# Two half-wide d_ff tiles in one PSUM bank, and three small moves of work between engines

## The chip, the cores and the metric

The kernel runs on one core of one Trainium2 chip. The metric is the device time of one execution in microseconds (us). The core has five engines with instruction streams of their own: TensorE (PE, with its weight loads shown as PEld), VectorE (DVE), ScalarE (ACT), GpSimd (POOL) and SyncE (SP), which here only issues transfers. Each works through its own stream in order and waits for the others through semaphores. TensorE writes its results to PSUM, from where ScalarE or VectorE must fetch them.

## The reference

Attention within chunks of 64 tokens, then a feed-forward layer with a squared relu (8 batches, 8 heads, 576 tokens a batch, head size 64; 4608 tokens, d_model 512, d_ff 2048):

```python
# q, k, v: [8, 8, 576, 64], cut into chunks of 64 tokens
scores = scale * q_c @ k_c.T          # within a chunk, scale = 1/8
attn = softmax(scores)
x = (attn @ v_c)                      # laid out as [4608 tokens, 512]
h = np.maximum(x @ w_in, 0.0)         # [4608, 2048]
out = (h * h) @ w_out                 # [4608, 512], float32
```

## The kernel before

Tokens are taken in 18 groups of 256 (`GT`), two groups to a block, so nine blocks of 512 tokens. For each block the kernel runs a feed-forward expansion (`ffn_in`) and a contraction (`ffn_out`, or `ffn_out_by_ft` in block 0). All products are in bf16.

**Expansion.** `ffn_in` goes over tiles of 128 columns of d_ff. A tile takes a bank of PSUM (`ps_ffn`, four buffers), four matmuls over d_model, a relu on ScalarE into the buffer `rl` (three buffers), and a square into `gT`. The square runs on VectorE, for a few named tiles on ScalarE (`SQUARES_ON_ACT`, `SQUARES_ON_ACT_EARLY`), so as to share the load. In blocks 2 to 8 a tile is 512 tokens wide and the tiles follow the order `FT_EARLY`: 8, 0, 9, 1, 10 to 15, 2 to 7, so tile 7 is the last. In block 1 the second group of tokens isn't ready when the block starts, so the tiles are 256 tokens wide: 16 tiles for the first group, 16 for the second, in the order 8 to 15, 0 to 7 (`FT_ORDER`).

**Contraction.** `ffn_out` multiplies with a scheme of seven products over quarters of `gT` and `w_out` (Strassen's, in Winograd's manner of sharing). It needs the differences d5, d2, d1, d6 and d7 of quarters of `gT`, which VectorE computes into `w_st` (the line of `difference`), and sums of quarters of `w_out`, made once (`sum_quarters`). The products use the order a22, a11, d5, d2, d1, d6, d7; d5 needs all of tiles 0 to 15 for the first group of tokens, tile 7 with them.

**Attention between the matmuls.** The attention of later groups is put into the blocks by a plan written by hand. Each `yield` of the expansion and the contraction ends a slot, and after slot s the plan emits the pieces listed for it. The pieces of a group are: C, which casts q and k to bf16 (`cast_qk`, on GpSimd for groups below 8, on ScalarE after); TD, which transposes them with a DMA on SP's queue; TA, TQ and TK, which transpose them on TensorE for the early groups; SC, scores and exp (`scores`); AV, the product with v and the division by the sum (`values`), whose reciprocal and multiplication are on VectorE and make `x`; XT, the transpose of x into `xT`, from which `ffn_in` reads (on TensorE for groups 2 to 5, by DMA later). Loads of q, k and v are issued on SP at the slots named in `go_slots`. As SP is in order, a load that is emitted behind a TD starts only after it, and TD waits for the casts of C.

In block 0's plan, TA, SC, AV and XT of group 2 stand at slots 24, 27, 29 and 31; slots 16 to 27 are `ffn_out_by_ft`'s tiles 0 to 11, slots 28 to 31 its last four token tiles. In block 1's plan, TK, SC, AV and XT of group 3 stand at slots 1, 4, 7 and 12, C of groups 4 and 5 at slots 16 and 20, TD at 21 and 27, their SC at 36 and 37 and AV at 38 and 40. From block 2 on, the two AV of the next block's groups stand near slots 11 and 15, which is the last slot of the expansion.

Of the kernel before, what the change touches and what calls it, by code (L numbers as in the profile page):

```python
# [10 lines left out]
FP32 = mybir.dt.float32  # L11
BF16 = mybir.dt.bfloat16
AF = mybir.ActivationFunctionType
ALU = mybir.AluOpType
# [3 lines left out]
def kernel(  # L18
# [9 lines left out]
    nc = tc.nc  # L28
# [24 lines left out]
    FIRST_DMA_T = 4  # L53
    FIRST_DMA_X = 6
    SQUARES_ON_ACT = (10, 14, 3)
    SQUARES_ON_ACT_EARLY = (9, 10, 12)
    BT = GT * max(len(b) for b in blocks)

    const_pool = ctx.enter_context(tc.tile_pool(name="const", bufs=1))
# [5 lines left out]
    ps_ffn = ctx.enter_context(tc.tile_pool(name="ps_ffn", bufs=4, space=bass.MemoryType.PSUM))  # L65
# [90 lines left out]
    def go(pieces):  # L156
        for f in pieces:
            f()
# [94 lines left out]
    def cast_qk(g):  # L253
        qkb = att_pool.tile([128, 2, 2 * H * D], BF16, name="qkb", bufs=2)
        state["qkb", g] = qkb

        copy = nc.gpsimd.tensor_copy if g < 8 else nc.scalar.copy
        q_sb, k_sb = (x.rearrange("p t h d -> p (t h d)") for x in qk[g])
        copy(  # L259
            out=qkb[:, 0].rearrange("p (i h d) -> p i h d", i=2, h=H),  # L260
            in_=q_sb.rearrange("p (h i d) -> p i h d", h=H, i=2))
        copy(out=qkb[:, 1], in_=k_sb)  # L262
# [90 lines left out]
    SC, AV, XT = scores, values, transpose_x  # L353
# [25 lines left out]
    def difference(j, name, part):  # L379
        if (name, j) not in state:  # L380
            state[name, j] = wst_pool.tile([128, 1024], FP32, name="w_st").bitcast(BF16).rearrange(
                "p (a f) -> p a f", a=HF)
        x, y = (quarters(j)[i][:, part] for i in DIFFERENCES[name])
        nc.vector.tensor_tensor(out=state[name, j][:, part], in0=x, in1=y, op=ALU.subtract)  # L384
# [4 lines left out]
    FT_EARLY = [ft + h for ft in range(N_EARLY) for h in (n_ft // 2, 0)]  # L389
    FT_EARLY += [ft for ft in FT_ORDER if ft not in FT_EARLY]  # L390

    def ffn_in(j, parts):
        if j not in gTs:
            gTs[j] = ffn_pool.tile([128, n_ft, BT], BF16, name="gT")
        gT, xT = gTs[j], xTs[j]
        for u, (c, n, fts, ft) in enumerate((*p, ft) for p in parts for ft in p[2]):
            h = ps_ffn.tile([128, 512], FP32, name="ps_ffn")
            for dt in range(n_dt):
                nc.tensor.matmul(  # L399
                    out=h[:, 0:n],  # L400
                    lhsT=w_in_bf[:, dt, ft * 128:(ft + 1) * 128],
                    rhs=xT[:, c // 128:(c + n) // 128, dt, :],
                    start=(dt == 0), stop=(dt == n_dt - 1))
            if j < 3:
                if n == 512 or u % 2 == 0:
                    rl_tile = ffn_pool.tile([128, 512], FP32, name="rl", bufs=3).bitcast(BF16)
                rl = rl_tile[:, u % 2 * 512:] if n < 512 else rl_tile
            else:
                rl = ffn_pool.tile([128, 512], FP32, name="rl", bufs=3)
            nc.scalar.activation(out=rl[:, 0:n], in_=h[:, 0:n], func=AF.Relu)  # L410
            on_act = SQUARES_ON_ACT_EARLY if fts is FT_EARLY else SQUARES_ON_ACT
            if (n == 512 and ft in on_act) or (n < 512 and (j == 0 or ft in (12, 3))):
                nc.scalar.activation(out=gT[:, ft, c:c + n], in_=rl[:, 0:n], func=AF.Square)  # L413
            else:
                nc.vector.tensor_tensor(  # L415
                    out=gT[:, ft, c:c + n], in0=rl[:, 0:n], in1=rl[:, 0:n], op=ALU.mult)
            if fts is FT_EARLY and u == 8:

                for name in ("d5", "d2", "d1", "d6", "d7"):
                    difference(j, name, slice(0, N_EARLY))  # L420
            yield
# [11 lines left out]
    def sum_quarters(out, in0, in1, op=ALU.add, half=slice(None)):  # L433
        return lambda _: add(nc.vector, out[:, half], in0[:, half], in1[:, half], op)
# [126 lines left out]
    def ffn_out_by_ft(j):  # L561

        gT = gTs.pop(j)
        n_tt = len(blocks[j]) * GT // 128
        o_ps = [ps_ffn.tile([128, d_model], FP32, name="ps_ffn") for _ in range(n_tt)]

        def mm(tt, ft):
            nc.tensor.matmul(  # L568
                out=o_ps[tt],
                lhsT=gT[:, ft, tt * 128:(tt + 1) * 128],  # L570
                rhs=w_out_bf[:, ft, :],
                start=(ft == 0), stop=(ft == n_ft - 1))


        for ft in range(n_ft - 4):
            for tt in range(n_tt - 1 if ft == 0 else n_tt):
                mm(tt, ft)
                if ft == 1 and tt == n_tt - 2:
                    mm(n_tt - 1, 0)
            yield  # L580
        for tt in range(n_tt):
            for ft in range(n_ft - 4, n_ft):
                mm(tt, ft)
            o_sb = ffn_pool.tile([128, d_model], FP32, name="o_sb", bufs=4)
            nc.scalar.copy(out=o_sb, in_=o_ps[tt])
            b, s0 = chunks[blocks[j][tt // 2]][0]
            t0 = b * S + s0 + tt % 2 * 128
            nc.gpsimd.dma_start(out=out[t0:t0 + 128, :], in_=o_sb)
            yield

    def pieces(grps):
        for g in grps:
            yield from qk_pieces(g)
        for g in grps:
            yield from v_pieces(g)
# [43 lines left out]
    for j, grps in enumerate(blocks):  # L639
        nxt = blocks[j + 1] if j + 1 < len(blocks) else []  # L640
        far = blocks[j + 2] if j + 2 < len(blocks) else []
        plan = {}

        def at(slot, f, g):
            plan.setdefault(slot, []).append((f, g))

        if j == 0:
            loads, go_slots = itertools.chain(*map(qk_pieces, far)), range(17)
            at(28, sum_quarters(b11_p_b21, b11, b21), None)
            for slot, f in ((24, TA), (27, SC), (29, AV), (31, XT)):  # L650
                at(slot, f, nxt[0])
            at(31, TQ, nxt[1])
            at(31, sum_quarters(b11_m_b22, b11, b22, ALU.subtract), None)
            phases = [first_ffn_in, ffn_out_by_ft(0)]
        elif j == 1:
            loads = itertools.chain(*map(v_pieces, nxt), *map(qk_pieces, far))
            go_slots = [*range(22, 27), *range(28, 48)]
            for slot, f in ((1, TK), (4, SC), (7, AV), (12, XT)):
                at(slot, f, grps[1])
            for i, g in enumerate(nxt):  # L660
                for slot, f in ((16 + 4 * i, C), (21 + 6 * i, TD), (36 + i, SC), (38 + 2 * i, AV),
                                (42 + i, XT)):
                    at(slot, f, g)
            for i, g in enumerate(far):
                at(36 + 4 * i, C, g)
                at(42 + 3 * i, TD, g)
            at(2, sum_quarters(b11_p_b12, b11, b12), None)
            at(12, sum_quarters(b12_p_b22, b12, b22), None)
            at(20, sum_quarters(b21_p_b22, b21, b22), None)
            phases = [ffn_in(1, [(0, 256, FT_ORDER), (256, 256, FT_ORDER)]), ffn_out(1)]  # L670
        else:
            loads, go_slots = pieces(far), range(32)
            slots = {SC: (8, 8), AV: (11, 15), XT: (14, 18), C: (18, 20), TD: (20, 23)}
            if j == 3:
                go_slots = [*range(6), *range(13, 32)]
            if j == 2:
                loads = itertools.chain(*map(v_pieces, nxt), loads)
                slots = {SC: (8, 10), AV: (12, 15), XT: (15, 18), C: (20, 23), TD: (22, 25)}
                go_slots = [*range(16), 23, 24, *range(26, 36)]
            for f in (SC, AV, XT):  # L680
                for i, g in enumerate(nxt):
                    at(slots[f][i], f, g)
            for f in (C, TD):
                for i, g in enumerate(far):
                    at(slots[f][i], f, g)
            phases = [ffn_in(j, [(0, BT, FT_EARLY)]), ffn_out(j)]
        slot = 0
        for phase in phases:
            for _ in phase:
                if slot in go_slots:  # L690
                    for f in loads:
                        f()
                        break
                for f, g in plan.get(slot, []):
                    f(g)
                slot += 1
        assert all(x < slot for x in plan), (j, slot, sorted(plan))
        go(loads)
# [30 lines left out]
```

The softmax here doesn't subtract the row's maximum and nothing guards it: scores larger than these inputs give would overflow.

## Time and profile before

| What | Value |
|---|---|
| Time, median of 3 runs | 282.13 us (281.37 to 282.69) |
| Span of the profiled execution | 281.0 us |
| TensorE busy | 269.7 us, 96% |
| VectorE busy | 189.6 us, 67% |
| ScalarE busy | 162.3 us, 58% |
| GpSimd busy | 48.5 us, 17% |
| Granted TensorE clock | full throughout |

Stages in the span: preparation and block 0 from 0 to 50.4 us, block 1's expansion to 68.1 and contraction to 83.4, block 2's expansion from there to 99.1, then about 28 us for each block, expansion and contraction, and the last block up to 281.0. The busy time of an engine is the time in which an instruction of it is being executed. Matmuls are pipelined, so their busy time says less than the idle time of the weight loads: where the next weights could not be loaded, or had to wait, TensorE stood still. In rows of the timeline the columns are start, duration, engine, line, operation, what it writes and reads, shapes and count; in brackets stands the idle time of that engine just before, with the instruction that ended it. In the table of windows each engine's busy time is given with the number of its instructions, and behind them the granted clock, the busy share of the DMA engines and GB/s.

### The profile page before, as it was taken

The numbers are of one execution on the slowest core, as the hardware profiler recorded it, in microseconds if no ns is written. First come the engines' busy times: TensorE is split into PE (matmuls) and PEld (weight loads), VectorE is DVE, ScalarE is ACT, GpSimd is POOL, SyncE is SP. The second block draws the span as 40 slices with busy tenths as digits, with TensorE's granted clock in tenths as the row PEclk, the third lists the DMA queues.
The fourth block names the chain that finished last, engine by engine and source line by source line (L and its number), as shares of the span: only waits on it lengthen the run. The fifth ranks groups of instructions, "written<-read, shape, count | busy, mean of one in ns | idle before, by whom it ended". The sixth has DMA issues, their size and how long they took to land.

```text
span 281.0 us, 7202 instructions
## 1 busy us (share of the span) xinstructions
PE 269.7 (96%) x2954; PEld 175.8 (63%) x2954; DVE 189.6 (67%) x338; ACT 162.3 (58%) x278; POOL 48.5 (17%) x79
## 2 busy tenths in 40 slices
PE   1999999999999999999999999999999999999995
PEld 1554454778884488448844884488448844884584
DVE  1255605798972795499549954995499549954983
ACT  1458705776438753977197719771977197219610
POOL 2038844150271000000000030003000300051000
PEclk9999999999999999999999999999999999999999
DMA  7999999999899999998899799669797970332003
GB/s 199 241 320 351 344 359 254 317 223 219 212 244 258 212 216 204 263 247 189 168 308 227 173 241 274 113 135 221 208 264 166 186 195 2 75 96 56 0 28 124
DMA packets 143072, 57.09 MB, mean 203 GB/s; under 512 B 110656, under 2 KB 140480, under 8 KB 143040
## 3 DMA queue, kind: packets, MB, share of 16 engines
q1 hardware_dynamic: 140768, 50.15, 77.4%
q0 software_dynamic: 1984, 6.29, 7.1%
q8 instruction: 23, 0.38, 0.6%
q10 hardware_dynamic: 288, 0.20, 0.2%
q14 instruction: 9, 0.07, 0.1%
HBM read 36.70 MB, written 9.44 MB: 164 GB/s over the span
## 4 chain that ended last, share of the span: by engine, by line
PE 62%; DVE 23%; ACT 8%; issue 3%; DMA 2%; SPq 0%; ACTq 0%
PE ps_ffn L468 29%; PE ps_ffn L399 22%; DVE gT L415 11%; ACT rl L410 6%; DVE x L326 6%; PE ps_ffn L568 5%; DVE w_st L384 5%; DMA k_sb<-in_k_dram 2%; PE ps_ffn L249 1%; PE ps_ffn L202 1%; PE ps_att L291 1%; DVE rec L325 1%; ACT gT L413 1%; PE ps_att L318 1%; PE ps_att L345 0%
## 5 line engine op out<-in xcount | busy, mean ns | idle before, releaser
L399 PE MATMUL ps_ffn<-xT,w_in_bf 128*128 128x512 bf16 (+1 forms) x648 | 129.6, 356 | 0.5 <-DVE xT L350 0.2
L415 DVE TENSOR_TENSOR gT<-rl 128x512 bf16<-128x512 f32 (+2 forms) x130 | 74.3, 608 | 53.6 <-ACT rl L410 53.3
L410 ACT ACTIVATE rl<-ps_ffn 128x512 f32<-128x512 f32 (+2 forms) x162 | 85.5, 549 | 22.5 <-PE ps_ffn L399 19.8
L399 PEld LDWEIGHTS <-w_in_bf 128*128 128x128 bf16 x648 | 61.7, 98 | 58.3 <-issue 0.6
L468 PEld LDWEIGHTS <-w_st 128*128 128x128 bf16 x640 | 61.8, 98 | 9.0 <-DVE w_st L384 1.8
L384 DVE TENSOR_TENSOR w_st<-gT 128x1536 bf16<-128x1536 bf16 (+2 forms) x75 | 50.3, 720 | 0.0
L468 PE MATMUL ps_ffn<-w_out_bf,w_st 128*128 128x256 bf16 x384 | 45.9, 273 | 0.4
L496 POOL DMA_DIRECT2D out_dram<-o_sb x16 | 11.5, 717 | 132.1 <-DVE o_sb L431 128.8
L468 PE MATMUL ps_ffn<-w_sum,w_st 128*128 128x256 bf16 x256 | 29.6, 273 | 0.0
L548 ACT COPY o_sb<-ps_ffn 128x512 f32<-128x512 f32 (+1 forms) x8 | 4.5, 560 | 40.9 <-PE ps_ffn L468 40.9
L468 PEld LDWEIGHTS <-gT 128*128 128x128 bf16 x256 | 24.5, 98 | 3.3
L326 DVE TENSOR_TENSOR x<-ps_att,rec 128x512 bf16<-128x512 f32 x36 | 24.9, 692 | 1.2
L302 ACT ACTIVATE e<-ps_att 128x1024 bf16<-128x1024 f32 x18 | 17.8, 1023 | 6.0 <-PE ps_att L291 6.0
L413 ACT ACTIVATE gT<-rl 128x512 bf16<-128x512 f32 (+2 forms) x32 | 18.5, 578 | 1.0
L468 PE MATMUL ps_ffn<-w_sum,gT 128*128 128x256 bf16 x128 | 15.3, 273 | 0.0
L468 PE MATMUL ps_ffn<-w_out_bf,gT 128*128 128x256 bf16 x128 | 15.3, 273 | 0.0
L568 PE MATMUL ps_ffn<-w_out_bf,gT 128*128 128x512 bf16 x64 | 14.5, 379 | 0.0
L170 POOL CAST w_in_bf<-w_st 128x512 bf16<-128x512 f32 (+2 forms) x12 | 9.9, 843 | 17.9 <-DMA w_st<-in_moe_w_in_dram 17.9
L512 ACT COPY n<-ps_ffn 128x512 f32<-128x512 f32 (+1 forms) x9 | 4.9, 539 | 12.0 <-PE ps_ffn L468 12.0
L318 PEld LDWEIGHTS <-e 64*64 64x64 bf16 x576 | 6.5, 107 | 7.4 <-ACT rl L410 2.5
L259 ACT CAST qkb<-q_sb 128x1024 bf16<-128x1024 f32 x10 | 10.5, 1049 | 0.0
L262 ACT CAST qkb<-k_sb 128x1024 bf16<-128x1024 f32 x10 | 10.5, 1047 | 0.0
(53 smaller groups left out, 157.5 us busy)
## 6 DMA issues: line engine op xcount, KB each, us to landing
q_sb<-in_q_dram SPq DMA_DIRECT2D x16, 512.0 KB, 6.8
k_sb<-in_k_dram SPq DMA_DIRECT2D x24, 256.0 KB, 6.1
out_dram<-o_sb POOLq DMA_DIRECT2D x20, 256.0 KB, 4.7
ve_sb<-in_v_dram SPq DMA_DIRECT2D x32, 128.0 KB, 4.2
w_st<-in_moe_w_in_dram SPq DMA_DIRECT2D x8, 512.0 KB, 6.2
w_st<-in_moe_w_out_dram SPq DMA_DIRECT2D x8, 512.0 KB, 5.6
vo_sb<-in_v_dram SPq DMA_DIRECT2D x24, 128.0 KB, 3.6
out_dram<-o_sb SPq DMA_DIRECT2D x9, 256.0 KB, 2.9
```

What stands on the lines that cost most here:

```text
L259: copy(out=qkb[:, 0].rearrange("p (i h d) -> p i h d", i=2, h=H), in_=q_sb.rearrange("p (h i d) -> p i h d", h=H, i=2))
L262: copy(out=qkb[:, 1], in_=k_sb)
L302: nc.scalar.activation(out=e_out, in_=s_in, func=AF.Exp, scale=scale)
L326: nc.vector.tensor_tensor(out=x[:, t].rearrange("p h a d -> p a h d"), in0=o[:, :, :, 0:D], in1=rec.to_broadcast([128, 2, n_hp, D]), op=AL ...
L384: nc.vector.tensor_tensor(out=state[name, j][:, part], in0=x, in1=y, op=ALU.subtract)
L399: nc.tensor.matmul(out=h[:, 0:n], lhsT=w_in_bf[:, dt, ft * 128:(ft + 1) * 128], rhs=xT[:, c // 128:(c + n) // 128, dt, :], start=(dt == 0) ...
L410: nc.scalar.activation(out=rl[:, 0:n], in_=h[:, 0:n], func=AF.Relu)
L413: nc.scalar.activation(out=gT[:, ft, c:c + n], in_=rl[:, 0:n], func=AF.Square)
L415: nc.vector.tensor_tensor(out=gT[:, ft, c:c + n], in0=rl[:, 0:n], in1=rl[:, 0:n], op=ALU.mult)
L468: nc.tensor.matmul(out=outs[t], lhsT=a[:, i, t * 128:(t + 1) * 128], rhs=b[:, i, :], start=(first and i == 0 and (last or t == 0)), stop=( ...
L496: dma.dma_start(out=out[t0:t0 + HT, col:col + HD].rearrange("(t p) d -> p t d", p=128), in_=o_sb.rearrange("p (t d) -> p t d", d=HD))
L568: nc.tensor.matmul(out=o_ps[tt], lhsT=gT[:, ft, tt * 128:(tt + 1) * 128], rhs=w_out_bf[:, ft, :], start=(ft == 0), stop=(ft == n_ft - 1))
```

## The change

There are four edits.

1. In block 1, two neighbouring 256-wide d_ff tiles are put into one bank of PSUM. The first tile of a pair fills the left half and yields, the second fills the right half, and then one relu and one square of 512 columns do for both. The square writes two tiles of `gT` at once. ScalarE squares the pairs that end in tiles 13 and 3, VectorE the others. This is for fewer and larger instructions on ScalarE and VectorE in the block that has small ones. The number of slots stays, so the plan of block 1 isn't shifted.
2. The casts of group 4 go from GpSimd to ScalarE (`4 < g < 8` in place of `g < 8`), to take GpSimd's work away from block 1's start.
3. The square of tile 7, the last of the expansion, goes from VectorE to ScalarE in blocks 2 to 8, so that VectorE comes sooner to the work queued behind it.
4. In block 0, SC, AV and XT of group 2 are each emitted a slot sooner, so that `xT` is ready sooner for block 1.

```diff
-    SQUARES_ON_ACT_EARLY = (9, 10, 12)
+    SQUARES_ON_ACT_EARLY = (9, 10, 12, 7)
...
-        copy = nc.gpsimd.tensor_copy if g < 8 else nc.scalar.copy
+        copy = nc.gpsimd.tensor_copy if 4 < g < 8 else nc.scalar.copy
...
+        pairs = j == 1
         for u, (c, n, fts, ft) in enumerate((*p, ft) for p in parts for ft in p[2]):
-            h = ps_ffn.tile([128, 512], FP32, name="ps_ffn")
+            second = pairs and u % 2
+            if not second:
+                h = ps_ffn.tile([128, 512], FP32, name="ps_ffn")
             for dt in range(n_dt):
                 nc.tensor.matmul(
-                    out=h[:, 0:n],
+                    out=h[:, n:2 * n] if second else h[:, 0:n],
...
+            if pairs and not second:
+                yield
+                continue
+            m = 2 * n if pairs else n
...
-            nc.scalar.activation(out=rl[:, 0:n], in_=h[:, 0:n], func=AF.Relu)
...
+            rl = rl[:, 0:m]
+            nc.scalar.activation(out=rl, in_=h[:, 0:m], func=AF.Relu)
+            dst = gT[:, ft, c:c + n]
+            if pairs:
+                dst, rl = gT[:, ft - 1:ft + 1, c:c + n], rl.rearrange("p (a n) -> p a n", a=2)
+                on_act = ft in (13, 3)
...
+            if on_act:
+                nc.scalar.activation(out=dst, in_=rl, func=AF.Square)
+            else:
+                nc.vector.tensor_tensor(out=dst, in0=rl, in1=rl, op=ALU.mult)
...
-            for slot, f in ((24, TA), (27, SC), (29, AV), (31, XT)):
+            for slot, f in ((24, TA), (26, SC), (28, AV), (30, XT)):
```

More of the change, by code (lines that the diff above doesn't have):

```diff
@@ L403, in ffn_in @@
                     start=(dt == 0), stop=(dt == n_dt - 1))
+            if pairs and not second:
+                yield
+                continue
+            m = 2 * n if pairs else n
             if j < 3:
-                if n == 512 or u % 2 == 0:
+                if m == 512 or u % 2 == 0:
                     rl_tile = ffn_pool.tile([128, 512], FP32, name="rl", bufs=3).bitcast(BF16)
-                rl = rl_tile[:, u % 2 * 512:] if n < 512 else rl_tile
+                rl = rl_tile[:, u % 2 * 512:] if m < 512 else rl_tile
             else:
                 rl = ffn_pool.tile([128, 512], FP32, name="rl", bufs=3)
[L410 to L413, printed above, removed]
-            else:
-                nc.vector.tensor_tensor(
-                    out=gT[:, ft, c:c + n], in0=rl[:, 0:n], in1=rl[:, 0:n], op=ALU.mult)
+            rl = rl[:, 0:m]
[4 more added lines that the diff above has]
+                on_act = ft in (13, 3)
+            elif n == 512:
+                on_act = ft in (SQUARES_ON_ACT_EARLY if fts is FT_EARLY else SQUARES_ON_ACT)
+            else:
+                on_act = True
+            if on_act:
+                nc.scalar.activation(out=dst, in_=rl, func=AF.Square)
+            else:
+                nc.vector.tensor_tensor(out=dst, in0=rl, in1=rl, op=ALU.mult)
             if fts is FT_EARLY and u == 8:
```

## The prediction, made before the result was known

> **What bounds the kernel now.** I read the busy line first, then the chain of waits, then the windows of one stage each, and last the timeline of the three places where TensorE stops.
>
> ```profile
> PE 269.7 (96%) x2954; PEld 175.8 (63%) x2954; DVE 189.6 (67%) x338; ACT 162.3 (58%) x278; POOL 48.5 (17%) x79
> ```
>
> TensorE is the bound: 96% of 281.0 us. A change that leaves its matmuls alone can win only the stops of TensorE. Windows of single stages show where they are (span, then busy us of PE, PEld, DVE, ACT, POOL):
>
> ```profile
> 50.40:68.30 17.90, 16.99 (x218) 13.96 (x219) 16.14 (x36) 14.50 (x39) 4.86 (x5) 1.00 1.04 253
> ...
> 83.40:99.10 15.70, 15.70 (x194) 7.24 (x192) 8.03 (x21) 12.93 (x22) 1.42 (x2) 1.00 0.95 229
> 111.50:127.20 15.70, 15.70 (x196) 7.53 (x195) 10.59 (x21) 13.12 (x22) 0.00 (x0) 1.00 1.03 243
> ```
>
> The first is block 1's expansion: 0.91 us without a matmul, and VectorE busy 16.1 of 17.9 us. The same phase of blocks 2 and 3 has no hole. In the timeline of block 1 the weight loads show each stop (start, duration, what; in brackets the idle time before and who ended it):
>
> ```profile
> 50.42 0.77 PEld L399 LDWEIGHTS <-w_in_bf 128*128 128x128 bf16 x8 [0.38 <-DVE xT L350]
> ...
> 55.41 0.34 PEld L318 LDWEIGHTS <-e 64*64 64x64 bf16 x32 [0.45 <-ACT e L302]
> ...
> 58.17 0.23 PEld L345 LDWEIGHTS <-x 128*128 128x128 bf16 x4 [0.29 <-DVE x L326]
> 59.01 0.23 PEld L345 LDWEIGHTS <-x 128*128 128x128 bf16 x4 [0.61 <-DVE x L326]
> ...
> 64.35 0.42 PEld L399 LDWEIGHTS <-w_in_bf 128*128 128x128 bf16 x4 [0.31 <-issue]
> 65.07 2.93 PEld L399 LDWEIGHTS <-w_in_bf 128*128 128x128 bf16 x27 [0.30 <-issue]
> ```
>
> A change between matmul kinds leaves 0.21 us even where nothing is late, so the AV stop costs 0.24 net. The stop at 50.42 costs about 0.3, the two at XT 0.7, the last two 0.6: some 1.8 us. Why VectorE is late there:
>
> ```profile
> 55.67 1.61 DVE L415 TENSOR_TENSOR gT<-rl 128x256 bf16<-128x256 bf16 x3 [0.56 <-ACT rl L410]
> ...
> 56.07 1.07 POOL L259 CAST qkb<-q_sb 128x1024 bf16<-128x1024 f32 x1 [5.42 <-DMA q_sb<-in_q_dram]
> ...
> 60.95 1.46 POOL L259 CAST qkb<-q_sb 128x1024 bf16<-128x1024 f32 x1 [1.33 <-DMA q_sb<-in_q_dram]
> ...
> 61.42 3.21 DVE L415 TENSOR_TENSOR gT<-rl 128x256 bf16<-128x256 bf16 x7
> ...
> 65.69 1.29 DVE L415 TENSOR_TENSOR gT<-rl 128x256 bf16<-128x256 bf16 x6
> ```
>
> With GpSimd quiet six squares take 1.29 us (0.215 each); while it casts, seven take 3.21 (0.46 each). The third place is the same in blocks 3 to 7, near 130.8, 158.8, 186.9, 214.9 and 242.9:
>
> ```profile
> 127.51 0.68 DVE gT L415
> ...
> 129.88 0.88 DVE w_st L384
> 130.80 8.69 PE ps_ffn L468 x78
> ```
>
> In this chain tile 7's square, then the second group's x, then the difference d5 run in turn on VectorE, and the third matmul of the d5 product waits: it starts at 130.80, the product's first at 130.35, at 0.11 apiece the third was due at 130.57. So 0.23 to 0.24 a block, 1.2 us over five.
>
> **What the Trainium skill says.** "SBUF — State Buffer", Who interferes with whom: a VectorE operation with two SBUF inputs contends with a GpSimd operation that reads SBUF; the first to issue holds the shared port and the other blocks fully. The trace agrees: of the three squares at 55.67, one lasts to 57.28, just past the cast's end at 57.14. "TensorE: Matmul & The Clock Gate", Part 1: a warm matmul of N columns issues every N/2.4 GHz plus 2.5 ns, 109 ns for 256; here 27 weight loads fill 2.93 us, 0.109 each. "PSUM — Partial Sum Buffer", PSUM bank collisions: guard by bank and quadrant, not by address; so a relu of a pair must wait for both tiles, which the program does, and no run here shows the other case. "DMA: Bandwidth & Descriptors", Anatomy of one DMA: a wait sits on the issuing sequencer, not in the DMA engines; the SP rows below agree.
>
> **The change part by part.**
>
> *Slot sooner in block 0.* SC, AV and XT of group 2 move from slots 27, 29, 31 to 26, 28, 30, each four 128x512 matmuls (4 x 0.216 = 0.87 us) earlier. The xT copy now ending at 50.37 ends near 49.5, while TensorE still has slot 31's matmuls and TQ, up to 50.05. The stop at 50.42 goes: 0.33 us. Inputs: the last V piece of group 2 landed at 45.90, AV would start at 46.0; the exp needs qkT at 43.2, SC would start at 43.8. Both just fit.
>
> *Pairs.* 32 relus and 32 squares of 256 columns become 16 and 16 of 512. ScalarE, back to back: relu 256 columns every 0.27 us (53.04, 53.32, 53.58), 512 columns every 0.50 (two in 1.10, the last lasting 0.60). 32 x 0.27 = 8.6 becomes 16 x 0.50 = 8.0; squares 4 x 0.32 become 4 x 0.54, +0.9. Net +0.3 on ScalarE. VectorE squares: 28 x 0.205 = 5.7 becomes 12 x 0.36 = 4.3, saving 1.4. A 2x256 output isn't in the trace: I take the flat 512 price (0.42 single; ScalarE 0.63), since the sum written as 8x256 takes 1.21 beside 1.22 for a flat 2048; the upper end, two instructions' time, is 0.57. Each bank now holds two tiles, so four banks let TensorE run 3.5 us ahead instead of 1.75.
>
> *Group 4's casts to ScalarE.* They leave GpSimd, which frees VectorE by the blocked part: 0.78 (square of 1.06, not 0.28) and 0.60 (0.88). They add 2 x 0.95 us to ScalarE, in its order behind the relus of slot 15.
>
> *Walk through block 1*, from 50.10. AV is at 54.6, the exp ends at 54.4: no stop, 0.24 gained. The square of tiles 14/15 waits for their relu, which now stands behind the exp and a pair square: it starts at 56.1, x follows at 56.7 to 57.4 and 57.5 to 58.2. TensorE reaches XT at 57.2 and leaves at 58.6 (now 59.2): its stop stays near 0.75, the longer relu granularity eating what the absent cast gave. ScalarE then: xT copy to 59.7, two relus, the casts 60.6 to 62.6, relus again from 62.5. TensorE needs the bank of the first of these at 63.4, freed at 63.1: no stop, and the two at 64 to 65 (0.6) go. Sum in block 1: 0.33 + 0.24 + 0.6 = 1.2 us. Its expansion ends at 66.9, not 68.1. The last relu ends near 68.0, d5 near 69.6; TensorE wants d5 at 70.4.
>
> *What waits behind the cast.* This is the added wait:
>
> ```profile
> 59.65 2.71 SPq L268 DMA_TRANSPOSE qkT<-qkb  x1
> ...
> 62.41 1.11 SPq L148 DMA_DIRECT2D ve_sb<-in_v_dram  x2
> ```
>
> SP's transpose of group 4 starts as the GpSimd cast ends (59.62). With ScalarE it starts near 62.7, three us later, and SP being in order, so do all loads behind it: V of groups 4 and 5, TD(5), q/k of 6 and 7. The consumers: SC(5) at 72.7 (now 73.9), TD(5) issued near 67.8 and landing 4.1 later (65.50 to 69.62 now), 71.9; AV(5) at 76.4, V landed by 75.6; SC(7) at 92.2, its transpose 88.9 now plus 2 to 2.5, 91.4; AV(6) at 94.4, V landed 93.2 now, 95.2 then in part. The lag shrinks a little because the DMA share has gaps (0.79 at 64 to 66, 0.69 at 70 to 72). So nearly all fits; AV(6) is the doubtful one. I cost it at nothing in the likeliest case and 0.5 to 1.5 us in a rival.
>
> *Tile 7's square to ScalarE*, blocks 2 to 8. VectorE loses 0.69 us before the second group's x; rec then waits only for AV, done at 126.9. d5 comes 0.6 to 0.9 us earlier, 0.2 is needed. ScalarE has 1.65 us idle before the n copy at 128.80 and puts the 0.63 us square at 127.2 to 127.8; the a11 product reads tile 7 after 129. All five waits go: 1.2 us. Blocks 2 and 8 had none: nothing there.
>
> Sum: 1.2 + 1.2 = 2.4 us; 282.13 - 2.4 = 279.7, rounded to 279.8.
>
> **The rivals.** (A) The loads behind the late transpose miss AV(6), SC(5) or the xT transposes of block 2 (now landing 107.3 for 111.3): a stop of 0.5 to 1.5 us, so 280.3 to 281.3, say 280.8. For it: SP rows back to back from 62.4 to 78; against: margins of 0.8 us at SC(5) and AV(5). (B) ScalarE becomes the bound in block 1. Its rows there add to about 16 of 17 us, so casts meeting relus could stop TensorE as VectorE did: block 1 yields only the 0.33, and 280.6. Against: double depth in PSUM. (C) Slower: the transposes pile up, stops pass from block 1 into blocks 2 and 3 for over 3 us, or pair squares run at a quarter of the rate: 283.8. For it: DMA share of 1.0 and more throughout; against: the gain of 1.2 us at tile 7 doesn't depend on it.
>
> **How the numbers follow.** Likeliest case 0.67, A 0.18, B 0.10, C 0.05. The low end is every stop in blocks 1 and 3 to 7 gone, about 3.1 us: 279.0, with a little for the spread of the times 278.9. The high end takes in A and B: 281.4. The 0.5% bound is 280.7: the likeliest case lies under it but for run spread (281.37 to 282.69 before), A and B lie astride it: faster 0.74, same 0.22, slower 0.04.
>
> **What would show it.** Right: no wait of PEld on DVE w_st in blocks 3 to 7; block 1's first matmul without a wait on xT; no stop in tiles 8 to 15 of its second half; VectorE near 12 us busy in its expansion; XT still waiting about 0.75 us. Wrong: a stop at SC(5), AV(5), AV(6) or block 3's start with a DMA as releaser, a wait on ScalarE's relu after the casts, or pair squares well over 0.42 us with GpSimd quiet.

## The result and the profile after

The changed kernel takes 285.31 us (median of 6 runs, 283.81 to 287.29) against 282.23 for the kernel before in the same comparison (281.37 to 282.71). The ratio is 1.0115 with a 95% interval of [1.0071, 1.0158]. It is slower, where the forecast was 279.8 us and faster. Here and below a time is the median of all executions, while a ratio leaves out those that ran over 1.5% above the fastest of their kernel. The profiled execution has a span of 283.2 us, 2.2 more than before.

The busy line of the page of after shows that TensorE's work stayed and VectorE's became less, 182.1 us in 315 instructions (before 189.6 in 338), while ScalarE's grew from 162.3 to 168.2 us.

```profile
PE 269.3 (95%) x2951; PEld 176.1 (62%) x2954; DVE 182.1 (64%) x315; ACT 168.2 (59%) x271; POOL 44.5 (16%) x77
```

What became more is waiting for transfers. In the chain that ended last, the share of DMA was 2% before and is 15% after. This is the chain of before by engine:

```profile
PE 62%; DVE 23%; ACT 8%; issue 3%; DMA 2%; SPq 0%; ACTq 0%
```

And this is that of after, by engine and by line:

```profile
PE 78%; DMA 15%; DVE 3%; ACT 1%; issue 1%; SPq 1%; POOL 0%; ACTq 0%
PE ps_ffn L403 37%; PE ps_ffn L483 28%; DMA qkT<-qkb 8%; PE ps_ffn L583 5%; DMA k_sb<-in_k_dram 4%; DMA xT<-x 4%; PE ps_att L318 2%; PE ps_att L291 2%; PE ps_ffn L249 1%; PE ps_ffn L202 1%; DVE w_sum L446 1%; DVE x L326 1%; PE ps_att L202 1%; PE ps_ffn L237 0%; DVE qkT L211 0%
```

The places that the prediction looked at did what it said. (The edit shifts lines: the expansion's matmul is L403, its relu L419, its squares L429 on ScalarE and L431 on VectorE, the contraction's matmul L483.) This is the timeline of after for block 1's expansion, with the columns as before:

```profile
50.21 0.77 PEld L403 LDWEIGHTS <-w_in_bf 128*128 128x128 bf16 x8
...
54.97 0.35 PEld L318 LDWEIGHTS <-e 64*64 64x64 bf16 x32 [0.21 <-ACT e L302]
...
58.54 0.23 PEld L345 LDWEIGHTS <-x 128*128 128x128 bf16 x4 [0.61 <-DVE x L326]
58.72 8.23 PEld L403 LDWEIGHTS <-w_in_bf 128*128 128x128 bf16 x76
...
61.78 1.07 ACT L262 CAST qkb<-k_sb 128x1024 bf16<-128x1024 f32 x1
...
62.88 1.42 SPq L268 DMA_TRANSPOSE qkT<-qkb  x1
...
67.60 2.03 SPq L268 DMA_TRANSPOSE qkT<-qkb  x1
...
74.35 0.34 PEld L291 LDWEIGHTS <-qkT 64*64 64x64 bf16 x32 [1.67 <-DMA qkT<-qkb]
```

The block starts without a wait on `xT`, AV shows only the 0.21 of a change of kind, and from 58.72 to 66.95 the weights of 76 matmuls follow each other without a hole: the two stops for a bank are gone. The expansion ends at 67.07, 1.06 us sooner than before. Then comes the last row. The scores of group 5 (SC(5)) need the transpose that SP issued at 67.60, and TensorE, which could have started them at 72.89, gets it at 74.35. (The row shows 1.67 us idle; in before, with nothing late, the same step shows 0.21, so that 1.46 us are lost.) The block's whole gain is lost in one stop, and 0.4 us more: SC(5) started at 73.94 before.

It isn't the only one. In the chain of waits of after (start, duration, what), these steps are DMA transposes for which TensorE stands at their end:

```profile
67.60 6.71 DMA qkT<-qkb
...
86.51 7.80 DMA qkT<-qkb
...
163.18 5.09 DMA xT<-x
...
219.81 4.84 DMA xT<-x
...
225.06 8.90 DMA qkT<-qkb
```

TensorE's lost time there, over what the same step takes where nothing is late, is 1.46 us at 74.35, 0.58 at 94.35, 0.32 at 168.32, 0.67 at 224.70 and 1.10 at 234.01: 4.1 us. Against it stand the 1.06 of block 1 and the 1.2 of the d5 waits in blocks 3 to 7, none of which is left. The difference, 1.9, is most of the 2.2 by which the spans differ.

Where the transposes become late is seen in the DMA share. This is the table of windows of after (span; busy us of PE, PEld, DVE, ACT, POOL; granted clock; DMA share; GB/s). A packet counts with its whole time in the window in which it starts, so that a share can be above 1:

```profile
62.00:64.00 2.00, 2.00 (x20) 1.79 (x19) 0.68 (x3) 2.00 (x4) 1.04 (x1) 1.00 0.00 0
64.00:66.00 2.00, 2.00 (x21) 1.78 (x20) 1.87 (x4) 1.97 (x5) 0.00 (x0) 1.00 1.14 258
```

And this is the same stretch before:

```profile
62.00:64.00 2.00, 2.00 (x21) 1.80 (x19) 2.00 (x5) 0.76 (x4) 1.45 (x2) 1.00 0.95 213
64.00:66.00 2.00, 1.74 (x15) 1.27 (x14) 2.00 (x7) 1.97 (x7) 0.00 (x0) 1.00 0.79 176
...
70.00:72.00 2.00, 2.00 (x21) 1.79 (x19) 1.42 (x3) 0.59 (x1) 0.00 (x0) 1.00 0.69 152
```

While SP stands before the transpose of group 4 (TD(4)) until ScalarE's cast ends at 62.85, it issues nothing, what it had issued earlier runs out, and the DMA engines move nothing for two microseconds. The other face of it is seen in what follows: compared with the trace of before, TD(4) is issued 3.2 us later, TD(5) 2.1 later and landed 4.7 later, TD(7) issued 3.8 later and landed 5.4 later, and the `xT` transposes of block 2 landed 3.7 and 4.9 later.

### The profile page after: what moved, and what is told of

It reads as the page before. It is cut to its first block, busy times and chain, and to the rows that moved or that the text cites. A ratio compares the mean times of both kernels' runs of the same rounds, so it can differ in the third digit from the quotient of the medians.

```text
span 283.2 us, 7155 instructions
## 1 busy us (share of the span) xinstructions
PE 269.3 (95%) x2951; PEld 176.1 (62%) x2954; DVE 182.1 (64%) x315; ACT 168.2 (59%) x271; POOL 44.5 (16%) x77
## 4 chain that ended last, share of the span: by engine, by line
PE 78%; DMA 15%; DVE 3%; ACT 1%; issue 1%; SPq 1%; POOL 0%; ACTq 0%
PE ps_ffn L403 37%; PE ps_ffn L483 28%; DMA qkT<-qkb 8%; PE ps_ffn L583 5%; DMA k_sb<-in_k_dram 4%; DMA xT<-x 4%; PE ps_att L318 2%; PE ps_att L291 2%; PE ps_ffn L249 1%; PE ps_ffn L202 1%; DVE w_sum L446 1%; DVE x L326 1%; PE ps_att L202 1%; PE ps_ffn L237 0%; DVE qkT L211 0%
## 5 line engine op out<-in xcount | busy, mean ns | idle before, releaser
L403 PE MATMUL ps_ffn<-xT,w_in_bf 128*128 128x512 bf16 (+1 forms) x648 | 129.3, 356 | 0.7 <-DMA xT<-x 0.7
L431 DVE TENSOR_TENSOR gT<-rl 128x512 bf16<-128x512 f32 (+1 forms) x107 | 66.5, 649 | 59.4 <-ACT rl L419 58.8
L403 PEld LDWEIGHTS <-w_in_bf 128*128 128x128 bf16 x648 | 61.5, 98 | 58.7 <-DMA xT<-x 1.2
L419 ACT ACTIVATE rl<-ps_ffn 128x512 f32<-128x512 f32 (+2 forms) x146 | 83.7, 589 | 22.5 <-PE ps_ffn L403 21.2
L483 PEld LDWEIGHTS <-w_st 128*128 128x128 bf16 x640 | 62.1, 98 | 7.3
L483 PE MATMUL ps_ffn<-w_out_bf,w_st 128*128 128x256 bf16 x384 | 45.1, 273 | 0.0
L483 PE MATMUL ps_ffn<-w_sum,w_st 128*128 128x256 bf16 x256 | 29.6, 273 | 0.0
L483 PEld LDWEIGHTS <-gT 128*128 128x128 bf16 x256 | 24.5, 98 | 3.3
L429 ACT ACTIVATE gT<-rl 128x512 bf16<-128x512 f32 (+2 forms) x39 | 23.7, 608 | 1.2
L483 PE MATMUL ps_ffn<-w_sum,gT 128*128 128x256 bf16 x128 | 15.3, 273 | 0.0
L483 PE MATMUL ps_ffn<-w_out_bf,gT 128*128 128x256 bf16 x128 | 15.3, 273 | 0.0
L262 ACT CAST qkb<-k_sb 128x1024 bf16<-128x1024 f32 x11 | 11.5, 1048 | 1.6 <-DMA k_sb<-in_k_dram 1.6
L291 PEld LDWEIGHTS <-qkT 64*64 64x64 bf16 x576 | 6.2, 110 | 9.2 <-DMA qkT<-qkb 3.8
L259 ACT CAST qkb<-q_sb 128x1024 bf16<-128x1024 f32 x11 | 11.5, 1048 | 0.3 <-DMA q_sb<-in_q_dram 0.3
```

What stands on the lines that cost most here:

```text
L259: copy(out=qkb[:, 0].rearrange("p (i h d) -> p i h d", i=2, h=H), in_=q_sb.rearrange("p (h i d) -> p i h d", h=H, i=2))
L291: nc.tensor.matmul(out=ps[64 * c:64 * c + 64, o0:o0 + 64], lhsT=qkT[64 * a:64 * a + 64, 1, t, hp, cols], rhs=queries(a, t, hp, p), start=T ...
L403: nc.tensor.matmul(out=h[:, n:2 * n] if second else h[:, 0:n], lhsT=w_in_bf[:, dt, ft * 128:(ft + 1) * 128], rhs=xT[:, c // 128:(c + n) // ...
L419: nc.scalar.activation(out=rl, in_=h[:, 0:m], func=AF.Relu)
L429: nc.scalar.activation(out=dst, in_=rl, func=AF.Square)
L431: nc.vector.tensor_tensor(out=dst, in0=rl, in1=rl, op=ALU.mult)
```

## The experiments

The theory after this reading (theory W): the casts on ScalarE hold SP, the queue behind it drains, and the lag stops TensorE. The rivals: ScalarE's own load in block 1 (S); the other edits, the pairs above all, which bring TensorE sooner to transfers that come no sooner (P); and late transposes that fall where they will and have nothing to do with the edits. Every ratio is against the kernel before on the same chip. Three groups of runs were made, with the kernel before at 282.34, 282.36 and 282.99 us.

### Only the casts back on GpSimd

```diff
-        copy = nc.gpsimd.tensor_copy if 4 < g < 8 else nc.scalar.copy
+        copy = nc.gpsimd.tensor_copy if g < 8 else nc.scalar.copy
```

(edits 1, 3 and 4 stay)

> The changed kernel with the casts of group 4 back on GpSimd; the other three edits stay. Theory W (the wait of SP's queue behind the ScalarE cast starves the DMA engines for 2 us and the lag is never made up): TD(4) issues near 59.6 again, no stop with a DMA as releaser over 0.3 us, and the time is 280.0 to 280.8, 1.5 to 2.2 us below the kernel before. Rival P (the other edits let TensorE run ahead of a DMA stream that was about to bound the kernel anyway): the stops on DMA stay, 282 to 284.

Measured: 281.44 us, ratio 0.9954 [0.9935, 0.9974]. Without this one edit the change is a gain, so the loss belongs to the casts. The gain is less than theory W said. The profiled execution is the slowest of the 22 (285.12 us), and its trace isn't free of stops: none at SC(5) or SC(7), but TensorE was idle for 0.76, 0.75 and 1.39 us before late transposes at 175.66, 224.61 and 234.21. Stops in the late blocks thus come without the late casts too.

### Only the casts moved

The kernel before with `4 < g < 8` and nothing else.

> The kernel before with the casts of group 4 on ScalarE and nothing else. Theory W: slower than before by 3 to 5 us, 285 to 287, with stops at SC(5) and in later blocks on transposes. Rival P: the cast alone costs at most 1 us, 282 to 283.

Measured: 283.69 us, ratio 1.0033 [1.001, 1.0057]: slower, but by far less than the 3 to 5 us of theory W and by less than the whole change. On top of the other three edits the same edit costs 1.1% (1.0063, measured below, against the 0.9954 of the first experiment). The timeline of this kernel shows another stop, on the same edit:

```profile
61.67 1.05 ACT L262 CAST qkb<-k_sb 128x1024 bf16<-128x1024 f32 x1
...
62.74 1.41 SPq L268 DMA_TRANSPOSE qkT<-qkb  x1
...
63.05 3.22 PE L399 MATMUL ps_ffn<-xT,w_in_bf 128*128 128x256 bf16 x28 [0.94 <-ACT rl L410]
```

With one tile to a bank, TensorE runs out of banks while ScalarE casts, and stands about 1 us for the relu behind them. The DMA engines ran dry here too (share 0.03 from 62 to 64 us). Held back by that stop, TensorE asks for SC(5) at 73.67, when TD(5), 2.0 us later than before, has landed at 73.27: no stop. So in these traces the two stops don't come together: with the pairs the first is gone, and TensorE then meets the second. Where the 0.9 us of this kernel are lost isn't seen here: its profiled execution was one of the faster (282.84 us), and since the two stops at XT are gone too, its contraction starts 0.27 us sooner than before.

### Only tile 7's square on ScalarE

The kernel before with `SQUARES_ON_ACT_EARLY = (9, 10, 12, 7)` and nothing else.

> The kernel before with tile 7's square on ScalarE in blocks 2 to 8 and nothing else. Theory W: the five waits on the difference d5 go, 1.2 us, so 281.0. Rival P: TensorE meets late transposes in blocks 5 and 7 (0.3 to 1.8 us), so 281.5 to 283.

Measured: 281.79 us, ratio 0.997 [0.9948, 0.9992]. All five waits for d5 are gone from its trace. The ratio stands for 0.85 us; the 1.2 us forecast (0.9957) lies within the interval, though the time itself falls into the range that rival P gave. One stop of this trace is on a transpose, with no change anywhere near the SP queue:

```profile
223.03 1.25 PE L399 MATMUL ps_ffn<-xT,w_in_bf 128*128 128x512 bf16 x5 [1.10 <-DMA xT<-x]
```

So stops in the late blocks, such as those at 168 to 234 us of after, come in single executions without the late casts also. Those at 74 and 94 us are another matter, as the repetition below shows. And TD(5) came late here too, issued at 67.25 and landed 5.91 us later, without a dry stretch ahead of it (DMA share 1.12 from 62 to 64 us); it stopped nothing, as TensorE came to SC(5) at 73.28.

### The wait taken away, the casts kept

In the changed kernel TD(4) is emitted behind the five V loads of group 4 instead of ahead of them, one slot before TD(5). SP then has these loads to issue while ScalarE casts:

```diff
-                for slot, f in ((16 + 4 * i, C), (21 + 6 * i, TD), (36 + i, SC), ...
+                for slot, f in ((16 + 4 * i, C), (26 + i, TD), (36 + i, SC), ...
```

> The changed kernel, casts on ScalarE, with TD(4) emitted at slot 26 instead of 21, so that the five V loads of group 4 stand ahead of it in SP's queue. Theory W: SP has loads to issue while it would have waited, the DMA engines don't run dry at 62 to 64 us, and the time falls to 280.0 to 281.5. A rival (the cast itself is at fault, through ScalarE's order or the later landing of the transpose, not the queue): it stays at 284 to 286.

Measured: 281.23 us, ratio 0.9944 [0.9916, 0.9972]. It lies in the range of theory W. The windows of this kernel:

```profile
62.00:64.00 2.00, 2.00 (x20) 1.80 (x19) 0.74 (x2) 2.00 (x4) 1.34 (x2) 1.00 0.81 175
64.00:66.00 2.00, 2.00 (x21) 1.79 (x20) 1.93 (x3) 1.97 (x5) 0.10 (x1) 1.00 1.11 239
```

ScalarE is as busy as in the changed kernel (2.00 and 1.97), the DMA engines stay fed (0.81 in place of 0.00), and no stop of TensorE on a transpose is left. TD(4) is even later than in the changed kernel (63.42), but TD(5) is issued at 65.50 and lands at 69.59. That takes ScalarE's load out as a cause and leaves what stood behind the wait: the V loads of group 4, and TD(5), which comes 2.1 us sooner than in the changed kernel.

### The changed kernel again

> The changed kernel once more, on the chip of these comparisons, to stand beside the others: 284 to 286, with a stop of 1 us or more at SC(5), released by the transpose TD(5).

Measured: 283.88 us (282.8 to 288.23), ratio 1.0063 [1.0035, 1.0092], overlapping the first measurement at its lower end and a little below the time that was said. Two rows of its timeline:

```profile
74.00 0.34 PEld L291 LDWEIGHTS <-qkT 64*64 64x64 bf16 x32 [1.41 <-DMA qkT<-qkb]
...
94.23 0.34 PEld L291 LDWEIGHTS <-qkT 64*64 64x64 bf16 x32 [1.23 <-DMA qkT<-qkb]
```

The stops at SC(5) and SC(7) are back in their places (1.20 and 0.80 us lost, DMA share 0.02 from 62 to 64), the late ones are not: one of 1.06 us at 169, none past 200. The first two came with the change both times; the number and size of the others belong to the single execution.

### A longer wait, with ScalarE free

Casts on GpSimd as in the first experiment, and between the cast of q and that of k of group 4, 17 clears of an unused tile on GpSimd. Nothing but these clears is added, and neither TensorE, ScalarE nor VectorE has an instruction more.

```diff
+            if g == 4:
+                for _ in range(17):
+                    nc.gpsimd.memset(idle, 0.0)
```

> The changed kernel with group 4's casts back on GpSimd, but 17 small memsets of an unused tile on GpSimd between the cast of q and the cast of k, so that the k cast ends near 62 us instead of 59.6. SP's queue then waits as it does in the changed kernel, while ScalarE has none of the casts. Theory W (the queue's wait is the cause): TD(4) issues near 62, the DMA engines run dry for 1 us or more, and the time is 283.5 to 285.5. Rival S (ScalarE's added work is the cause): 281.0 to 282.

Measured: 286.94 us, ratio 1.0177 [1.0141, 1.0213], more than either theory said. The windows of this kernel show four microseconds without transfers:

```profile
62.00:64.00 2.00, 2.00 (x21) 1.78 (x20) 1.20 (x3) 1.34 (x3) 1.77 (x6) 1.00 0.03 7
64.00:66.00 2.00, 2.00 (x21) 1.79 (x19) 2.00 (x2) 1.97 (x4) 2.00 (x3) 1.00 0.03 6
```

and its timeline the stop in the same place, longer:

```profile
63.57 1.04 POOL L266 CAST qkb<-k_sb 128x1024 bf16<-128x1024 f32 x1
...
64.63 1.41 SPq L272 DMA_TRANSPOSE qkT<-qkb  x1
...
76.02 0.34 PEld L295 LDWEIGHTS <-qkT 64*64 64x64 bf16 x32 [2.40 <-DMA qkT<-qkb]
```

Against the first experiment, which lacks only the clears, that is 5.5 us more (0.9954 there). Against the changed kernel, with TD(4) 1.8 us later and the casts on another engine, it is 286.94 - 283.88 = 3.1 us more. So the harm comes with ScalarE free as well: what counts is when SP is let go, not which engine casts.

The size needs care, for not all of it is waiting for transfers. Eight matmuls of one kind take 1.05 us just after the long stop, and eight more a microsecond later nearly twice that:

```profile
76.40 1.05 PE L487 MATMUL ps_ffn<-w_out_bf,w_st 128*128 128x256 bf16 x8
...
77.98 1.89 PE L487 MATMUL ps_ffn<-w_out_bf,w_st 128*128 128x256 bf16 x8
```

The granted clock was 0.50 from 77.3 to 80.7 us of this trace, which cost TensorE 1.4 us; no stop in the traces of the changed kernel, 1.46 us at most, was followed by such a stretch. In five of this kernel's six executions the mean granted clock was 0.994, in 14 of the 16 of the changed kernel 0.998 or more. So some 1.4 of the 3.1 us is the clock. The clears also weren't without effect ahead of the stop: the two idle times at XT were 0.69 and 0.62 us (after: 0.26 and 0.61).

### Only the pairs

The kernel before with edit 1 alone.

> The kernel before with the pairs of block 1 and nothing else (casts on GpSimd). If pairs alone free TensorE of the two waits on a bank at 64 to 65 us, at the price of a longer wait at XT: 282.0 to 282.4, the same as before. If the pairs were worth the 0.9 us of my walk: 281.3.

Measured: 282.53 us, ratio 1.0007 [0.9982, 1.0032]: no difference that this can tell. In its trace the bank stops are gone, and 0.9 us of stops on transposes at 94.24 and 168.67 stand in their place, though the casts are on GpSimd and the DMA engines don't run dry (share 1.11 from 62 to 64). In this execution GpSimd itself began the cast of group 4 late (58.54, before 56.07), behind a stop of 1.5 us in block 0, and TD(4) was issued at 62.34. What the pairs win is lost again to transfers in this execution; here rival P has its part.

### The best order, group 2 at its old slots

The fourth experiment with edit 4 undone (SC, AV, XT of group 2 at 27, 29, 31).

> As the run with TD(4) behind the V loads, but SC, AV and XT of group 2 at their old slots 27, 29 and 31 in block 0. There AV(2) waited about 0.6 us for the V loads of group 2 where the xT copy had cost 0.3. If the slot sooner only traded one wait for another: 281.0 to 281.3, no slower than that run; if it was worth its 0.33 us: 281.5 to 281.7.

Measured: 280.67 us (280.36 to 281.41), ratio 0.9952 [0.993, 0.9975], below both ranges that were said. With edit 4 the ratio was 0.9944: the edit does nothing that can be measured. In the trace with it, TensorE waits at AV of group 2 for V, around 46.4 and 46.8 us, 0.7 us in all, and in that without it is idle for 0.38 us before `xT` comes at 50.45. One wait was put in the place of another. This version is one to keep: faster than the kernel before and than the changed kernel, though the first and fourth experiments (0.9954 and 0.9944) can't be told from it.

### Do the casts on ScalarE earn anything?

The eighth experiment with the casts on GpSimd again (`g < 8`).

> The changed kernel with group 4's casts on GpSimd again, its transpose behind the V loads, and group 2's pieces at their old slots: pairs and tile 7 alone, with the new order of the SP queue. Tells whether the casts on ScalarE earn anything once their wait is out of the way. If they do (VectorE freed of two blocked squares in block 1): 281.3 to 282, above the version with them on ScalarE (280.7), with a stop of some 0.5 us at XT or a bank in block 1. If the whole gain is that of tile 7's square and of an early transpose: 280.5 to 280.9, the same within the interval.

Measured: 282.89 us, against 282.99 for the kernel before; that comparison scattered more (280.47 to 287.02 and 281.5 to 288.56), and its ratio is 0.9967 [0.9937, 0.9996]. The interval overlaps that of the eighth experiment; no worth of the casts on ScalarE is shown, nor is one excluded. The profiled execution had the shortest span of all, 278.8 us, no stop on a transpose, and idle times of 0.35 and 0.62 us at XT.

### Only the order of the SP queue

The kernel before with `(26 + i, TD)` and nothing else.

> The kernel before with nothing but the order of the SP queue changed: the transpose of group 4 behind the V loads, at the slot after them. If the order is itself a gain (the V loads of group 4 and the transpose of group 5 no longer wait for GpSimd's cast, and late transposes stop TensorE less): 281 to 281.8, ratio 0.996 to 0.998. If the order only undoes the harm of the casts on ScalarE: 282.0 to 282.6, the same as before within the interval.

Measured: 282.85 us, ratio 0.9995 [0.9965, 1.0025]. As far as this can tell, the order is no gain of its own. It undoes the harm of the late casts.

Side by side, from the traces (times in us; TD(5) took is from issue to landing; a dash where the landing isn't recorded):

| Kernel | TD(4) issued | TD(5) issued | TD(5) took | SC(5) starts | TensorE lost there |
|---|---|---|---|---|---|
| before | 59.65 | 65.50 | 4.12 | 73.94 | 0 |
| after | 62.88 | 67.60 | 6.71 | 74.35 | 1.46 |
| after again | 62.80 | 67.54 | – | 74.00 | 1.20 |
| casts back | 60.47 | 66.49 | 4.27 | 73.73 | 0 |
| casts only | 62.74 | 67.49 | 5.78 | 73.67 | 0 |
| tile 7 only | 61.81 | 67.25 | 5.91 | 73.28 | 0 |
| pairs only | 62.34 | 67.52 | – | 74.35 | 0 |
| longer wait | 64.63 | 69.31 | 6.66 | 76.02 | 2.19 |
| TD behind V | 63.42 | 65.50 | 4.09 | 73.43 | 0 |
| best order | 63.53 | 65.99 | 3.91 | 73.12 | 0 |
| best order, casts on GpSimd | 63.42 | 65.78 | 3.85 | 73.06 | 0 |
| order only | 63.16 | 66.29 | – | 72.71 | 0 |

## Why the prediction was wrong

**Right.** The bank stops and the AV stop went, and block 1's expansion ended at 67.07 (said: 66.9). The XT stop stayed, with some 0.7 us (said: 0.75). VectorE is busy 12.10 us in the expansion (said: near 12), the pair square takes 0.42 us with GpSimd quiet, as a flat one. All five d5 waits went, and alone that edit is a gain of a size that fits. ScalarE isn't the bound (rival B).

**Right, but without effect.** The slot sooner did remove the wait for `xT`, counted with 0.33 us. The inputs "both just fit", the prediction said. V didn't: in after TensorE is idle for 0.16 us at AV of group 2, and the fourth and eighth experiments show no difference with and without the edit.

**The step that failed** is "What waits behind the cast", which the prediction cost "at nothing in the likeliest case". It named the waiting instruction, the queue behind it and the consumers, and gave them the right order. TD(4) was issued at 62.88 (said: near 62.7) and TD(5) at 67.60 (said: 67.8), and TensorE could have started SC(5) at 72.89 (said: 72.7). AV(6), the consumer that it doubted, had no wait. Two terms of its sum were mis-sized.

The first is "landing 4.1 later". That was the duration of this one transpose in the trace of before, where TD(6) and TD(7) took 6.37 and 6.13, and TD(5) now took 6.71 us. The table shows that those issued by 66.5 us took 3.9 to 4.3 us and those issued from 67.25 on 5.8 to 6.7. So the margin of 0.8 us became a stop of 1.46.

The second is "the lag shrinks a little because the DMA share has gaps". It grew: at TD(7) the issue was 3.8 us late instead of 2 to 2.5, and the landing at 94.31 instead of 91.4. A gap of 0.79 or 0.69 in the share of before was read as room for catching up, though rival C took the same share to be 1.0 and more throughout. But the stalled queue made a gap of its own, of two microseconds at share 0.00, and the prediction didn't ask what the DMA engines do while SP stands. The Trainium skill's page that it cited, "DMA: Bandwidth & Descriptors" (Anatomy of one DMA), says that a wait sits on the issuing sequencer. The runs here agree (SP issued nothing until 62.88, and the share was 0.00 from 62 to 64), and the consequence, DMA engines that run out of work behind the one instruction, should have been drawn.

**The rivals.** Rival A named the place, a DMA stop at SC(5), and was too small: 0.5 to 1.5 us for all, where SC(5) and SC(7) alone lost 2.0 in both traces of the changed kernel. Rival C had the size (283.8 us, of which 283.88 and 285.31 were measured) and the mechanism, transposes that pile up and pass stops into later blocks. It was given 0.05, with the argument that tile 7's 1.2 us doesn't depend on it. That is true, and no argument against 4 us of new stops. The gain made it worse, as the 0.33% of the casts alone beside the 1.1% on top of the other edits show: a TensorE that comes sooner needs the late transfers sooner, and the margins of the kernel before came with its own stops.

**Open.** That holding SP's queue does the harm is shown by three runs (casts back, TD behind V, longer wait). By which of two ways isn't: the dry stretch itself, or the later issue of TD(5), which with tile 7 alone took 5.91 us without a dry stretch. The kernel before has one trace, and with the same queue and casts TD(4) was issued at 60.47, 61.81 and 62.34 in three other traces. So a part of the lags read against the one trace may be that execution's own. Why the lag isn't made up sooner (in block 3, up to 146 us, transposes still landed 1.8 to 4.5 us late) is read from the DMA share, which is near 1 on most of the way, and wasn't tested by a run with fewer transfers. How much of the late stops (168 to 234 us) of the first trace belongs to the lag isn't separated from chance; the repetition had fewer.

## What to carry to other kernels

Before moving work to another engine, find who waits for its result, and if that is an in-order queue of transfers, list what stands behind it: a wait there can idle the DMA engines (two microseconds here), and where these are near full, the lag can stay for long: here transposes were still 4.9 us late 45 us on. If the waiting transfer isn't the first one needed, put it behind the others; here that turned a loss of 0.6 to 1.2% into a gain of 0.5%. Don't take the margins of the kernel before for the new one when TensorE itself comes sooner, and give a transfer's landing a range, not the one duration that the trace happens to show.

## What the runs showed of the hardware

The length of a DMA transpose went with what else was in flight. The profile's page counts a small queue of instruction fetches and one of the stores that GpSimd issues (queue and kind; packets, MB, share of 16 engines; the page of after):

```profile
q0 software_dynamic: 1984, 6.29, 7.5%
q8 instruction: 23, 0.38, 0.6%
```

The records of packets give, for all transposes after 55 us in the traces of the kernel before, the changed one and nine of the ten experiments (all but the first) together:

```
from issue to landing, us: number, lowest, median, highest
transpose of q and k   no fetch, no stores       43   3.81  4.14   4.86
                       a fetch of 8 or 16 KB     32   4.03  5.39   6.71
                       80+ packets of stores     18   4.88  6.08   8.93
                       both                      53   4.77  7.50  10.76
transpose of x         no fetch, no stores       77   3.07  3.32   4.00
                       a fetch of 8 or 16 KB     42   3.07  4.62   5.92
                       80+ packets of stores     10   4.50  4.78   5.63
```

(No stores means fewer than 80 packets of them.) An instruction fetch of 16 KB lasted 0.9 to 1.5 us in after. In after, one began at 69.3 us, in the middle of TD(5); packets of 256 bytes then took up to 1.8 us, where 0.03 to 0.07 was the most in the three microseconds before, and from 70 to 71 us only 19 packets started. In the kernel before the fetch at this place of the program came at 70.7, when TD(5) had landed. That would explain the 6.7 us, and the step between 66.5 and 67.25 in the table above: in the four traces where TD(5) took 5.8 us or more a fetch fell into its flight, in the five where it took 4.3 or less none did. It is a correlation found in the traces, in which a longer transpose also has more chance to meet a fetch; no run was made to test it.
